# Loading the first two pairs' queries and keys without zeros, and the first loads from one queue

## The chip, the cores and the metric

The program runs on one core of one Trainium2 chip. The metric is device time in microseconds (us) of one execution. TensorE (PE) multiplies, VectorE (DVE), ScalarE (ACT) and GpSimd (POOL) do the elementwise work, and SyncE (SP) issues transfers. SP and ACT each have a queue of transfers of their own; both are served by the same 16 DMA engines.

## The reference

Chunked attention (chunks of 64 rows), and then a mixture of experts on its output:

```python
scores = scale * np.matmul(q_c, k_c.transpose(0, 1, 2, 4, 3))   # (8, 8, 9, 64, 64)
scores = scores - np.max(scores, axis=-1, keepdims=True)
attn = np.exp(scores)
attn = attn / (np.sum(attn, axis=-1, keepdims=True) + 1e-09)
out = np.matmul(attn, v_c)
...
x = np.ascontiguousarray(attn_out.transpose(0, 2, 1, 3)).reshape(B * S, H * D)   # 4608 x 512
expert_idx = np.argmax(x @ w_gate, axis=1)
...   # the 80 tokens of highest gate weight of each of 8 experts
h = np.maximum(x[tok_idx] @ w1[e], 0.0)
out[tok_idx] = gate_w[tok_idx, None] * (h @ w2[e])
```

The change touches only how the first scores are loaded and computed.

## The kernel before

The attention is cut into 18 *pairs* (`NPAIR`); a pair is two tiles of 128 token rows by all 8 heads. For pair n the program runs, in this order of dependence:

- `load_qk(n)`: the queries and keys, 1 MB, in two transfers of 512 KB, into one of three buffers `qb0` to `qb2` (`NB` = 3). The heads' 64 features stand interleaved on even and odd partitions, so that one product with 128 contracted rows gives the scores of two heads. For that the buffer has three stretches of 512 columns, and half the partitions of the two outer stretches hold zeros, written once at the start by `memset`.
- `load_v(n)`: the values, 0.53 MB, in two transfers of 260 KB into `vb0` to `vb2`, whose other halves are zeros too.
- `scores(n)` (L331): 16 products of 128 rows x 64 columns of weights by 128 moving columns in float32, into the PSUM tile `s` (two banks). The trace has two records for each float32 product, so 32 for a pair. Pair 1 borrows the tile tagged `o`.
- `maxima(n)` and `minus(n)` (L348, L353) on DVE, `probs(n)` (L363: 16 transposes on PE into `pt`, then an exponential on ACT into `pT`), `values(2n)`, `values(2n+1)` (L391, into `o`), `divide`, `store` (to `xs`), `xtrans` (L363, `px`), and the gating products (L443).

The loop runs over n and writes the order out by hand, under a manual schedule: each engine does its instructions in the order of the code. In pass n, PE does `scores(n)`, then `xtrans(n-3)`, `values` of pair n-2 and `probs(n-1)`. The loads of pair n+3 are issued on SP in pass n after `scores(n)`, since they go into the buffer that `scores(n)` has just read. A later product on PE therefore waits for whatever stands ahead of it there, and a later transfer for whatever stands ahead of it on SP's queue.

Ahead of the loop stand 25 dummy products (`warm_up(NWARM)`, 128x256 in bfloat16, L664), which use a zeroed tile; pass 1 has 8 more after `probs(0)`. Pair 0 is special: its queries and keys come from `qk0`, an array made in advance that has the zeros in it, in two transfers of 768 KB, one issued by SP and one by ACT (L647). Also at the start SP and ACT share the loads of pairs 1 and 2 and of the first two values; the identity `ident` (64 KB, L648), which `probs` needs, goes on ACT's queue; the other constants go on SP's queue in pass 0. Some lines that the change and the prediction speak of:

```python
for t, eng in enumerate((nc.sync, nc.scalar)):
    eng.dma_start(qbufs[0][:, t], qk0[t])
nc.scalar.dma_start(ident, cst[:, C_ID:C_ID + P])
for j, eng in ((1, nc.vector), (2, nc.gpsimd)):
    eng.memset(qbufs[j][:, :, 0:512], 0.0)
    eng.memset(qbufs[j][:, :, 1024:1536], 0.0)
```

After pair 17 come a selection of tokens (PE, DVE, short dependent steps with dummy products `pwarm`, L620, between them), a gather of the selected rows from `xs` (`xgc`), and the experts: `hc` (L201) and `yc` (L234) on PE, while SP loads 2 MB weights (L905) into buffers as they come free. The expert weights' buffers `w1_0` and `w2_0` (tags `w1`, `w2`) lie empty until pass 15, where `early_weights` begins to fill them.

## Time and profile before

| what | value |
|---|---|
| median of 3 runs | 243.59 us (243.24 to 244.13) |
| profiled execution, its own time | 243.36 us |
| its span (first to last instruction) | 241.6 us |
| PE busy | 222.9 us (92% of the span) |
| DVE, ACT, POOL busy | 114.8, 66.6, 56.6 us |
| moved by DMA | 85.24 MB, mean 353 GB/s |
| on the chain that ended last | PE 85%, DMA 6%, DVE 4% |

The span is 1.8 us shorter than the execution's own time. A busy share is a mean over the program; what a change at the start is worth is read from the first microseconds and from whether PE has idle time behind them.

### The profile page before, as it was taken

Reading aid. Unit: us, or ns where it says so; the run is one execution under the profiler, and the core shown is the slowest. Engines: PE = TensorE matmul, PEld = TensorE weight load, DVE = VectorE, ACT = ScalarE, POOL = GpSimd, SP = SyncE. Lnnn points to the kernel's source line nnn. Section 1 sums busy time; section 2 is a strip of 40 time slices with the busy share of each in tenths; the row PEclk is TensorE's granted clock in tenths of the full one; section 3 lists DMA queues with packets and bytes.
Section 4 is the critical chain, followed back from the end, with each engine's and each line's share of the span. In section 5 each row is a group of like instructions: output and inputs, shape, how many; then the busy total and the mean of one; then the engine's idle time right before and its main releaser. Section 6 shows DMA issues by size and latency. Waiting matters only on the chain.

```text
span 241.6 us, 7213 instructions
## 1 busy us (share of the span) xinstructions
PE 222.9 (92%) x3126; PEld 143.5 (59%) x3126; DVE 114.8 (48%) x250; ACT 66.6 (28%) x117; POOL 56.6 (23%) x158
## 2 busy tenths in 40 slices
PE   8599999999999999989799399999999999999970
PEld 5498988988898898878568233433334333343310
DVE  6468869687878778787586401111211112011210
ACT  0213535363645455454632011201102002010000
POOL 9200400222323222229584620000000000000361
PEclk9999999999999999999979769999999999999997
DMA  6999999999999996989999989999999999999141
GB/s 251 406 382 399 391 407 407 409 410 404 385 379 348 363 346 226 352 322 296 298 409 414 349 250 379 398 407 414 411 401 410 416 408 417 399 403 381 74 151 41
DMA packets 34742, 85.24 MB, mean 353 GB/s; under 512 B 3025, under 2 KB 3153, under 8 KB 34705
## 3 DMA queue, kind: packets, MB, share of 16 engines
q1 hardware_dynamic: 32880, 79.40, 87.0%
q0 software_dynamic: 960, 2.88, 3.5%
q10 hardware_dynamic: 864, 2.43, 2.6%
q8 instruction: 26, 0.43, 0.7%
q14 instruction: 12, 0.09, 0.1%
HBM read 64.53 MB, written 20.45 MB: 352 GB/s over the span
## 4 chain that ended last, share of the span: by engine, by line
PE 85%; DMA 6%; DVE 4%; issue 1%; ACT 1%; POOL 0%; POOLq 0%; DVEq 0%; ACTq 0%
PE hc L201 18%; PE yc L234 17%; PE o L391 14%; PE s L338 13%; PE px L363 5%; PE pt L363 5%; PE small L443 4%; DMA qb<-in_qk 3%; DMA xgc<-xs,gic 3%; PE hpc L219 3%; PE pwarm L620 2%; PE xpc L189 1%; PE small L453 1%; PE small L563 1%; PE two L821 1%
## 5 line engine op out<-in xcount | busy, mean ns | idle before, releaser
L201 PE MATMUL hc<-w,xtc 128*32 128x512 f32 x384 | 45.1, 611 | 0.0
L234 PE MATMUL yc<-w,htc 128*32 128x512 f32 x384 | 42.3, 592 | 0.0
L338 PE MATMUL s<-qb 128*64 128x128 f32 x576 | 35.4, 276 | 2.8 <-DMA qb<-in_qk 2.6
L391 PE MATMUL o<-vb,pT 128*64 128x130 f32 x576 | 36.1, 276 | 0.0
L338 PEld LDWEIGHTS s<-qb 128*64 128x64 f32 x576 | 31.1, 137 | 5.6 <-DVE mx L348 2.4
L391 PEld LDWEIGHTS o<-vb,pT 128*64 128x64 f32 x576 | 31.5, 135 | 1.2
L348 DVE TENSOR_REDUCE mx<-s 128x16 f32<-128x1024 f32 x18 | 22.0, 1225 | 16.7 <-PE s L338 16.6
L234 PEld LDWEIGHTS yc<-w,htc 128*32 128x32 f32 x384 | 12.4, 110 | 28.3 <-issue 28.3
L201 PEld LDWEIGHTS hc<-w,xtc 128*32 128x32 f32 x384 | 12.7, 112 | 26.8 <-issue 25.1
L372 ACT ACTIVATE pT<-pt 128x1024 f32<-128x1024 f32 x18 | 18.4, 1024 | 30.6 <-PE pt L363 30.6
L253 POOL DMA_INDIRECT out<-ysc,to x6 | 6.0, 993 | 88.9 <-SPq L920 86.6
L434 ACT COPY xT<-px 128x1024 f32<-128x1024 f32 x17 | 17.1, 1007 | 22.8 <-PE px L363 22.8
L406 DVE TENSOR_TENSOR x<-o,rc 128x1024 f32<-128x1024 f32 (+1 forms) x20 | 22.4, 1118 | 0.7
L353 DVE TENSOR_TENSOR sm<-s,mx 128x1024 f32<-128x1024 f32 x18 | 22.1, 1227 | 0.6
L206 ACT ACTIVATE hsc<-hc 128x512 f32<-128x512 f32 x6 | 3.6, 598 | 64.9 <-PE hc L201 64.9
L239 DVE TENSOR_SCALAR ysc<-yc,gatec 128x512 f32<-128x512 f32 x6 | 4.5, 751 | 33.5 <-PE yc L234 33.5
L208 DVE TENSOR_SCALAR hsc<-hc 128x512 f32<-128x512 f32 x6 | 4.2, 692 | 26.2 <-PE hc L201 26.2
L223 DVE COPY htc<-hpc 128x512 f32<-128x512 f32 x6 | 4.1, 691 | 22.2 <-PE hpc L219 22.2
L363 PE MATMUL pt<-ct,sm 64*128 64x64 f32 x288 | 12.8, 229 | 1.2 <-ACT pT L372 1.2
L363 PEld LDWEIGHTS pt<-ct,sm 64*128 64x128 f32 x288 | 10.4, 139 | 4.3 <-issue 3.0
L363 PE MATMUL px<-ct,x 64*128 64x64 f32 x288 | 12.8, 229 | 0.0
L543 ACT ACTIVATE lv<-io_b,bo 128x256 bf16<-128x256 bf16 x29 | 12.5, 497 | 0.4 <-DVE bo L523 0.4
(136 smaller groups left out, 210.4 us busy)
## 6 DMA issues: line engine op xcount, KB each, us to landing
w<-in_w SPq DMA_DIRECT2D x12, 2048.0 KB, 18.9
qb<-in_qk SPq DMA_DIRECT2D x32, 512.0 KB, 6.8
out<-zero SPq DMA_DIRECT2D x9, 1024.0 KB, 16.2
vb<-in_vv SPq DMA_DIRECT2D x34, 260.0 KB, 6.4
xs<-x SPq DMA_DIRECT2D x16, 512.0 KB, 6.1
w<-in_w SPq DMA_DIRECT2D x16, 512.0 KB, 7.2
qb<-in_qk ACTq DMA_DIRECT2D x2, 512.0 KB, 8.6
xs<-x SPq DMA_DIRECT2D x4, 256.0 KB, 5.5
```

Of the source, the lines that this page charges most:

```text
L201: nc.tensor.matmul(h[o:o + 32, :], lhsT=xT[r][:, b, o:o + 32], rhs=getw(groups[r][g])[0][:, b, 512 * f:512 * f + 512], start=(b == 0), sto ...
L234: nc.tensor.matmul(y[o:o + 32, :], lhsT=hT[r][c // 4][:, c % 4, o:o + 32], rhs=getw(groups[r][g])[1][:, c, :], start=(c == 0), stop=(c == ...
L338: nc.tensor.matmul(ps[64 * u:64 * u + 64, t, P * pr:P * pr + P].rearrange("p (h k) -> p h k", h=2), lhsT=t8[:, 1, pr, u, :], rhs=t8[:, 0:3 ...
L348: nc.vector.tensor_reduce(d['mx'], d['s8'], axis=AX.X, op=ALU.max)
L353: nc.vector.tensor_tensor(d['sm'].rearrange("p c k h -> p h c k"), d['s8'], d['mx'][:, :, :, None].to_broadcast([P, 2, 8, 64]), op=ALU.sub ...
L363: nc.tensor.transpose(pm[:, u, 64 * c:64 * c + 64], src(c)[rows], ident[rows, rows])
L372: nc.scalar.activation(d['pT'], pt, AF.Exp, scale=0.125)
L391: nc.tensor.matmul(po[64 * u:64 * u + 64, o:o + 130].rearrange("p (h x) -> p h x", h=2), lhsT=d['pT'][:, u, c:c + 64], rhs=v[:, :, pr, u, ...
L406: nc.vector.tensor_tensor(TT[T][:, r:r + nt, :].rearrange("p r (k h e) -> p (r k) h e", k=4, h=2), pov[..., 0:64], rc[:, :, :, None].to_br ...
L434: nc.scalar.copy(dst, pm)
L443: nc.tensor.matmul(pl[32 * j:32 * j + 32], lhsT=wgp[:, pr], rhs=xt[:, 4 * (j % 2) + pr, :], start=pr == 0, stop=pr == 3, tile_position=(0, ...
L543: nc.scalar.activation(lv, io_b, AF.Sign, bias=bo[:, rt:rt + 1], scale=-1.0)
```

## The change

- Pairs 0 and 1 are no longer loaded into `qb0` and `qb1` but, without zeros, into the still empty buffers of expert 0's weights: pair 0 into `w1_0`, pair 1 into `w2_0`, each as two transfers of 512 KB (one for each of the two tiles of rows, `t`). The array `qk0` is gone.
- Their scores are made by 32 products instead of 16: 64 contracted rows x 64 columns of weights by 64 moving columns, at row halves h and column halves u. The scores' tile is laid out by head (`p h (c k)`), and `maxima` and `minus` read it so. The products of t = 0 wait only for the first transfer.
- All loads of the start are issued by SP in the order of use: pair 0, pair 1, `ident`, pair 2, values 0, pair 3, values 1, pair 4, values 2, and then the other constants. Pairs 3 and 4 need not wait for `scores(0)` and `scores(1)` any more. ACT issues none.
- The `memset`s of the buffers are dealt out anew: DVE writes half of `qb2`, `vb0`, both halves of `qb1`; POOL the other half of `qb2`, `qb0`, `vb1`, `vb2`.
- 16 dummy products at the start instead of 25, and 8 more behind `scores(1)`.

The core of the diff:

```diff
-NWARM = 25
+NWARM = 16
...
+        weights[0] = tiles_w(wp, 0)
+        first = {0: weights[0][0][:, 0:2],
+                 1: weights[0][1][:, 0:4].rearrange("p (t w) d -> p t (w d)", t=2)}
+
+        def load_qk(n):
+            if n in first:
+                for t in range(2):
+                    nc.sync.dma_start(first[n][:, t], qk[n, t])
+                return
             for h in range(2):
-                engs[h].dma_start(qbufs[n % NB][h:P:2, :, 512 * h:512 * h + 1024],
+                nc.sync.dma_start(qbufs[n % NB][h:P:2, :, 512 * h:512 * h + 1024],
                                   qk[n, :, 64 * h:64 * h + 64].rearrange("t p f -> p t f"))
...
+            if n in first:
+                for t in range(2):
+                    t8 = first[n][:, t].rearrange("p (w a u s) -> p w a u s", w=2, a=4, u=2)
+                    for pr in range(4):
+                        c = 64 * (4 * t + pr)
+                        for h in range(2):
+                            rows = slice(64 * h, 64 * h + 64)
+                            for u in range(2):
+                                nc.tensor.matmul(
+                                    ps[64 * u:64 * u + 64, h, c:c + 64],
+                                    lhsT=t8[rows, 1 - h, pr, u, :], rhs=t8[rows, h, pr, u, :],
+                                    start=True, stop=True)
+                return
...
-            for t, eng in enumerate((nc.sync, nc.scalar)):
-                eng.dma_start(qbufs[0][:, t], qk0[t])
-            nc.scalar.dma_start(ident, cst[:, C_ID:C_ID + P])
-            for j, eng in ((1, nc.vector), (2, nc.gpsimd)):
-                eng.memset(qbufs[j][:, :, 0:512], 0.0)
-                eng.memset(qbufs[j][:, :, 1024:1536], 0.0)
-            for j, vb in enumerate(vbufs):
-                (nc.vector, nc.gpsimd, nc.gpsimd)[j].memset(vb, 0.0)
+            load_qk(0)
+            load_qk(1)
+            nc.sync.dma_start(ident, cst[:, C_ID:C_ID + P])
+            for j, engs in ((2, (nc.vector, nc.gpsimd)), (0, (nc.gpsimd,) * 2),
+                            (1, (nc.vector,) * 2)):
+                for c, eng in zip((0, 1024), engs):
+                    eng.memset(qbufs[j][:, :, c:c + 512], 0.0)
+                (nc.vector if j == 2 else nc.gpsimd).memset(vbufs[(2, 0, 1).index(j)], 0.0)
             nc.vector.memset(wgp[:, :, 8:32], 0.0)
-            both = (nc.sync, nc.scalar)
-            load_qk(1, both)
-            load_qk(2, both)
-            load_v(0, both)
-            load_v(1, both)
+            for n in range(NB):
+                load_qk(2 + n)
+                load_v(n)
+            nc.sync.dma_start(ct[:, C_ID + P:], cst[:, C_ID + P:])
+            nc.sync.dma_start(wgp[:, :, 0:8], wg.rearrange("(b p) e -> p b e", p=P))
+            nc.sync.dma_start(capi, cap[0:1, :].broadcast_to([P, 2]))
...
                 scores(n)
-                if n + NB < NPAIR:
+                if n == 1:
+                    warm_up(8)
+                if 2 <= n < NPAIR - NB:
                     load_qk(n + NB)
-                    if n == 0:
-                        nc.sync.dma_start(ct[:, C_ID + P:], cst[:, C_ID + P:])
-                        nc.sync.dma_start(wgp[:, :, 0:8], wg.rearrange("(b p) e -> p b e", p=P))
-                        nc.sync.dma_start(capi, cap[0:1, :].broadcast_to([P, 2]))
-                        load_v(2)
```

PE before, from the end of the 25 dummy products to the first of pass 1's eight. `s_159` and `s_187` are the scores of pairs 0 and 1, `qb_99` and `qb_100` the buffers `qb0` and `qb1`, `pt_206` the transposes of pair 0, `ct` holds the identity; `DMAHW0` to `DMAHW7` are the semaphores that the transfers use in turn, and the other waits are for an engine.

```order
L338 MATMUL s_159<-qb_99 64x128 [waits DMAHW1_49]
L338 MATMUL s_159<-qb_99 64x128 x7
L338 MATMUL s_159<-qb_99 64x128 [waits DMAHW0_49]
L338 MATMUL s_159<-qb_99 64x128 x7
L338 MATMUL s_187<-qb_100 64x128 [waits DMAHW4_49,DMAHW3_49,DVE_49]
L338 MATMUL s_187<-qb_100 64x128 x15
L363 MATMUL pt_206<-ct,sm_185 128x64 [waits DMAHW2_49,DVE_49]
L363 MATMUL pt_206<-ct,sm_185 128x64 x15
```

PE of the change, from the end of its 16 dummy products. `s_163` and `s_200` are the scores of pairs 0 and 1, `w_0_102` and `w_0_103` the weights' buffers `w1_0` and `w2_0`.

```order
L350 MATMUL s_163<-w_0_102 64x64 [waits DMAHW0_49]
L350 MATMUL s_163<-w_0_102 64x64 x15
L350 MATMUL s_163<-w_0_102 64x64 [waits DMAHW1_49]
L350 MATMUL s_163<-w_0_102 64x64 x15
L350 MATMUL s_200<-w_0_103 64x64 [waits DMAHW2_49]
L350 MATMUL s_200<-w_0_103 64x64 x15
L350 MATMUL s_200<-w_0_103 64x64 [waits DMAHW3_49]
L350 MATMUL s_200<-w_0_103 64x64 x15
L687 LDWEIGHTS warm
L687 MATMUL small<-warm 128x256
```

Twice the products, each pair in two halves that wait for one transfer each, no wait for DVE's zeros ahead of pair 1, and a first dummy product where the transposes of pair 0 stood (they now follow the eight dummy products, and eight more follow them).

SP before, its first transfers. `vb_102` and `vb_103` are the values' buffers.

```order
L647 DMA qb_99<-in_qk 128x1536
L320 DMA qb_100<-in_qk 64x2x1024 [waits DVE_49]
L320 DMA qb_101<-in_qk 64x2x1024 [waits Pool_49]
L328 DMA vb_102<-in_vv 64x2x520 [waits DVE_49]
L328 DMA vb_103<-in_vv 64x2x520 [waits DMAHW1_49,Pool_49]
L320 DMA qb_99<-in_qk 64x2x1024 [waits DMAHW3_49,DMAHW0_49,PE_49]
```

SP of the change, its first transfers.

```order
L325 DMA w_0_102<-in_qk 128x1024 x2
L325 DMA w_0_103<-in_qk 128x1024 x2
L670 DMA ct<-in_cst 128x128
L328 DMA qb_101<-in_qk 64x2x1024 [waits DVE_49]
L328 DMA qb_101<-in_qk 64x2x1024 [waits Pool_49]
L336 DMA vb_104<-in_vv 64x2x520 [waits DVE_49]
L336 DMA vb_104<-in_vv 64x2x520 [waits DMAHW0_49]
L328 DMA qb_99<-in_qk 64x2x1024 [waits DMAHW1_49,Pool_49]
L328 DMA qb_99<-in_qk 64x2x1024 [waits DMAHW2_49,Pool_49]
```

SP now issues both halves of each load, the first five wait for nothing, and from the ninth transfer on each waits for the one eight places ahead of it to land. `qb_99` (pair 3) no longer waits for PE.

## Rows read from the trace of the kernel before

**Rows 1.** Chain of waits, first 21 us: start us, length us, what.

```profile
2.08 0.92 DVE qb L651
3.02 7.96 DMA qb<-in_qk
11.12 1.97 PE s L338 x32
13.09 0.65 PE pt L363 x16
13.74 0.98 PE small L664 x8
14.71 1.92 PE s L338 x32
...
17.92 1.23 DVE sm L353
...
19.25 1.97 PE s L338 x32
```

**Rows 2.** Windows: us, then busy us of PE, PEld, DVE, ACT, POOL; clock, DMA share, GB/s.

```profile
0.00:4.00 4.00, 2.91 (x14) 2.04 (x15) 2.45 (x3) 0.00 (x0) 3.47 (x8) 1.00 0.49 158
4.00:8.00 4.00, 3.64 (x32) 2.51 (x31) 1.27 (x2) 0.00 (x0) 3.38 (x6) 1.00 1.02 416
8.00:12.00 4.00, 1.81 (x34) 1.60 (x32) 2.45 (x2) 1.79 (x3) 0.00 (x0) 1.00 1.02 408
12.00:16.00 4.00, 4.00 (x68) 3.48 (x66) 2.45 (x2) 1.02 (x1) 0.00 (x0) 1.00 1.06 406
16.00:20.00 4.00, 3.78 (x74) 3.50 (x72) 3.24 (x5) 0.93 (x1) 0.00 (x0) 1.00 1.03 356
20.00:25.00 5.00, 5.00 (x99) 4.52 (x96) 4.33 (x6) 1.58 (x3) 0.00 (x0) 1.00 1.02 395
30.00:40.00 10.00, 10.00 (x195) 8.96 (x189) 7.55 (x12) 4.15 (x6) 0.00 (x0) 1.00 1.04 408
94.00:96.00 2.00, 2.00 (x46) 1.93 (x44) 1.88 (x6) 1.42 (x3) 0.23 (x2) 1.00 0.30 66
```

**Rows 3.** Timeline, first 18 us: start us, length, engine, line, what, count, idle before.

```profile
1.09 5.51 PE L664 MATMUL small<-warm 128*128 128x256 bf16 x25 [1.09 <-POOL warm L645]
3.38 1.79 DVE L653 MEMSET vb<- 128x2080 f32 x1 [0.38 <-issue]
...
6.96 1.97 PE L338 MATMUL s<-qb 128*64 128x128 f32 x32 [0.36 <-DMA qb<-in_qk]
...
8.98 1.22 DVE L348 TENSOR_REDUCE mx<-s 128x16 f32<-128x1024 f32 x1 [3.71 <-PE s L338]
...
13.67 1.05 PE L664 MATMUL small<-warm 128*128 128x256 bf16 x8
```

**Rows 4.** DMA view, first 1.3 us: issues, KB each, us to landing.

```profile
qb<-in_qk SPq DMA_DIRECT2D x1, 768.0 KB, 6.2
qb<-in_qk ACTq DMA_DIRECT2D x1, 768.0 KB, 6.4
```

**Rows 5.** Line L320, ACT's second issue (pair 2): issue, then issue to landing.

```profile
L320 ACTq DMA_DIRECT2D qb<-in_qk x1: 614/614/614, 3.8 to 3.8; - x1
...
DMA to landing us min/median/max: 9.2/9.2/9.2
```

**Rows 6.** Line L320, SP's issue at 11.0 us (pair 3, second half).

```profile
L320 SPq DMA_DIRECT2D qb<-in_qk x1: 602/602/602, 11.0 to 11.0; - x1
...
DMA to landing us min/median/max: 7.9/7.9/7.9
```

**Rows 7.** Chain of waits, later pieces: gating products, the gather, the experts.

```profile
29.53 1.01 PE small L443 x32
...
131.53 7.30 DMA xgc<-xs,gic
...
140.09 5.17 PE hc L201 x32
...
154.31 3.57 PE hc L201 x32
...
210.74 3.67 PE hc L201 x32
```

**Rows 8.** Windows: the two stretches of half clock, and the experts.

```profile
122.75:126.16 3.41, 3.39 (x17) 2.17 (x16) 2.82 (x5) 0.81 (x3) 2.92 (x8) 0.50 1.02 408
136.40:143.20 6.80, 4.19 (x20) 1.50 (x24) 0.60 (x4) 0.74 (x2) 3.35 (x5) 0.50 0.80 238
160.00:210.00 50.00, 50.00 (x464) 17.22 (x456) 6.40 (x9) 5.28 (x9) 0.00 (x0) 1.00 1.04 411
```

**Rows 9.** Waits of SP's queue: waiting line, what ended it, total us, times, longest.

```profile
SPq L905 <- DVE w L904: 14.9, 2, 14.5
```

More of the change, by code (lines that the diff above doesn't have):

```diff
@@ L54, in attention_moe @@
 @with_exitstack
-def attention_moe(ctx: ExitStack, tc: tile.TileContext, qk, qk0, vv, wg, w1, w2, cap, cst, out):
+def attention_moe(ctx: ExitStack, tc: tile.TileContext, qk, vv, wg, w1, w2, cap, cst, out):
     nc = tc.nc
@@ L316, in attention_moe @@
                  for j in range(NB)]
-        def load_qk(n, engs=(nc.sync, nc.sync)):
+        weights[0] = tiles_w(wp, 0)
[6 more added lines that the diff above has]
+                return
             for h in range(2):
-                engs[h].dma_start(qbufs[n % NB][h:P:2, :, 512 * h:512 * h + 1024],
+                nc.sync.dma_start(qbufs[n % NB][h:P:2, :, 512 * h:512 * h + 1024],
                                   qk[n, :, 64 * h:64 * h + 64].rearrange("t p f -> p t f"))
@@ L324, in attention_moe, with load_v @@
                  for j in range(NB)]
-        def load_v(n, engs=(nc.sync, nc.sync)):
+        def load_v(n):
             for h in range(2):
-                engs[h].dma_start(vbufs[n % NB][h:P:2, :, h],
+                nc.sync.dma_start(vbufs[n % NB][h:P:2, :, h],
                                   vv[n, :, h].rearrange("t p f -> p t f"))
@@ L346, in maxima @@
             d['mx'] = wk.tile([P, 2, 8], F32, name=f"mx{n}", tag="mx")
-            d['s8'] = d['s'].rearrange("p t (c h k) -> p h (t c) k", h=2, k=64)
+            d['s8'] = (d['s'].rearrange("p h (c k) -> p h c k", k=64) if n in first else
+                       d['s'].rearrange("p t (c h k) -> p h (t c) k", h=2, k=64))
             nc.vector.tensor_reduce(d['mx'], d['s8'], axis=AX.X, op=ALU.max)
@@ L632, in early_weights @@
             e, c = divmod(n, 8)
-            if c == 0:
+            if n == 8:
                 weights[e] = tiles_w(wp, e)
@@ L1044, in _arrays @@
         [np.where(f, k, q), np.where(f, q, k)], -1).reshape(NPAIR, 2, P, QK))
-    a = r["qk"][0].reshape(2, 2, 64, QK)
-    z = np.zeros((2, 64, 2, QK + 512), a.dtype)
-    z[:, :, 0, :QK], z[:, :, 1, 512:] = a[:, 0], a[:, 1]
-    r["qk0"] = z.reshape(2, P, QK + 512)
     r["vv"] = np.ascontiguousarray(t.reshape(NPAIR, 2, 2, 64, VW))
```

## Prediction

> **What bounds the kernel now.** I read the windows first, to see whether PE ever has time to make up a late or early start. It has none: from 30 to 40 us and from 160 to 210 us PE is busy for the whole stretch, and so it is already from 12 us on, but for a moment near 19 us [rows 2, 8]. So what happens before PE's row of work begins goes one for one into the end. Then the chain of waits shows where that row begins [rows 1]. Zeros written by DVE until 3.0 us hold back a load of pair 1 that ACT issues; it lands at 10.98 (3.02 + 7.96), and from its landing on everything is PE: scores of pair 1 at 11.12, transposes of pair 0, eight dummy products, scores of pair 2 at 14.71. Scores of pair 3 come 4.54 us later, held by DVE's subtraction for pair 2. Ahead of 11 us PE has idle time: 1.81 of 4 us busy from 8 to 12 [rows 2]. **The mark I follow is the start of pair 2's scores, 14.71 us**; behind it the order of work is the same before and after.
>
> The second thing is the DMA. It moves 416, 408, 406 GB/s from 4 to 16 us, full [rows 2]. So the landings of the start are bytes in order over this rate, and I need their curve.
>
> **The curve of the bytes.** From rows 2 (GB/s by length): 0.63 MB by 4 us, 2.30 by 8, 3.93 by 12, 5.55 by 16, 6.98 by 20. A transfer has landed somewhat after the bytes up to its own are through, since later ones run beside it. Three landings give that lag. Pair 0 (2 x 0.79 = 1.57 MB) lands at 0.72 + 6.2 to 6.4 = about 7.0 [rows 4], where the curve has 1.88: lag 0.3 MB. Pair 2 lands at 3.8 + 9.2 = 13.0 [rows 5] with 4.33 MB moved; ahead of it and with it stand 1.57 + 0.07 + 1.05 + 1.05 = 3.74: lag 0.6. Pair 3 lands at 18.9 [rows 6] with 6.58 moved against 5.85 (another 1.05 and two values of 0.53): lag 0.7.
>
> **Loads after.** In the new order the sums in MB are: pair 0 0.52 and 1.05, pair 1 1.57 and 2.10, identity 2.16, pair 2 3.21, values 3.74, pair 3 4.79, values 5.33, pair 4 6.38, values 6.91. With the lag they land, by the curve, at about 4.4 and 5.7, 7.2 and 8.5, 8.7, **11.5 (pair 2)**, 13.0, 15.8, 17.4, 20.3, 22. Pair 2 comes 1.5 us earlier than before, nearly all of it the 0.52 MB of zeros no longer loaded (1.3 us at 0.41 MB/us). SP's own time does not bind: nine issues at 0.6 us each [rows 5] end by about 6 us, while the bytes of the first eight last until 13. Waiting for the transfer eight places ahead leaves over 2 MB, some 5 us, in the queues.
>
> **PE after.**
> - *Dummy products.* 16 instead of 25 at 0.22 us [rows 3] end at 1.09 + 3.5 = 4.6 us. Nothing is saved by that on the path, since pair 0's first half lands at 4.4; kept at 25 they would hold pair 0 until 6.6, and it would still be done about when pair 1 lands.
> - *The 64-row products.* The trace has none. Bounds for a pair (64 records): the same columns stream as in 32 records of 128 columns, which take 1.97 us [rows 3]; the gating products take 1.01 us for 32 records of a quarter of the columns of the array [rows 7], so 2.0 for 64; if two row halves ran beside each other as the column halves do, 1.0; if each record cost what a 128-column one does, 3.9. Two rows say 2.0, and I take it: 1.0 for a half.
> - *Pair 0* is done at 5.7 + 1.0 = 6.7. DVE's zeros, now 3 x 0.92 + 1.79 + 0.14, with gaps, end near 6.2 and just miss being late. Maxima and subtraction (1.22 + 1.23 [rows 1, 3]) are ready at 9.2, the identity at 8.7, both over 1 us ahead of the transposes below.
> - *Pair 1* is done at 8.5 + 1.0 = 9.5. Behind it stand eight dummy products (0.98), the transposes of pair 0 (0.65), eight dummy products (0.98) [rows 1]: 2.6 us, **pair 2's scores at 12.1**. The new eight are a cost of 1 us on the path, partly covered: without them the transposes would start at 9.5 and pair 2 at its landing, 11.5.
> - *Behind it*, by the spacing of before: values 0 at 13.8 (landed 13.0), pair 3 at 16.6 (15.8), values 1 at 19.3 (17.4), pair 4 at 21.7 (20.3). Each load is there, pair 3 and values 0 by only 0.8 us. The constants go from ahead of values 2 to behind it and land near 23; the first to want them is ACT's copy near 23, which nothing on PE waits for at once.
>
> **The sum.** 14.71 - 12.1 = 2.6 us earlier. The other edits (layout of the scores, POOL's zeros, which gate only loads that land after 11 us) are hidden behind the loads. The profiled execution took 243.36: 243.36 - 2.6 = 240.8. The median of the runs is 0.23 above it, so **241.0 us**. With products at 1.0 us for a pair the chain is 11.6, just behind pair 2's landing: 3.1 us, 240.5. With 3.9 it is 13.1: 1.6 us, 242.0.
>
> TensorEngine Tiling (Array Packing) of the Trainium skill, section Tiling Modes, says that 64x64 tiles are four independent ones that load and multiply in parallel. By it the products take the 1.0 us end and the time is 240.5; no run here shows it.
>
> **Does the gain last to the end?** The DMA has room before the experts (share 0.30 from 94 to 96 us [rows 2]), so its stream moves with PE. The experts' weights are loaded once the gather has landed (the wait of 14.5 us [rows 9]), and the gather moves along too.
>
> **Rivals.**
> - *The clock, which is also the case that ends slower.* The first 25 dummy products take 0.22 us each, the later eight 0.13 [rows 3]. 256 columns at 1.2 GHz are 0.21 us, at 2.4 GHz 0.11: PE starts at the lower level, though the window prints 1.00, and has risen by pair 0's scores, 1.97 us as in all later pairs. Before, 5.5 us of unbroken work stood ahead of the rise. Now 3.5 us do, and then halves of pairs with gaps for loads. If PE is still at 1.2 GHz through pair 1, its half costs 2.0 and not 1.0, and part of the dummy products doubles: 1 to 1.6 us lost, 242.0 to 242.6. At half clock up to pair 2's scores the chain is 8.5 + 2 x 3.6 = 15.7, 1.0 later than before: 244.6. It decides near 14 us: a rise later than that makes the kernel slower, by half of every further us. For it: PE stands at 0.50 in two later stretches, one of them behind its wait for the gather [rows 7, 8]. Against: the gap of over 2 us before pair 1 did not bring it down [rows 2, 3]. TensorE: Matmul & The Clock Gate of the Trainium skill, Part 1, has the throttled state as the default, released by sustained activity at a point that differs between runs; that speaks against cutting the warm-up, and the trace's slow start agrees. 0.16 for the small loss, 0.04 for slower.
> - *The loads decide.* If pair 2 lands no earlier than before (13.0), because one queue starts slower than two, the scores start at 13.1 and the gain is 1.6: 242.0. For it: pair 2, pair 3 and values 0 have under 1 us to spare. Against: from 30 to 40 us SP alone carries 408 GB/s. 0.10.
> - *Given back in the experts.* The DMA carries 411 GB/s from 160 to 210 us, and one piece of `hc` at 210.74 takes 3.67 instead of 3.57 us [rows 7, 8]: a weight comes just in time. If that stream did not move, PE would wait for it there and the time would be 243.5. Against it stands what I said of the gather. 0.08.
> - *Luck behind the start.* Pieces at half clock (5.17 us instead of 3.57 for `hc` [rows 7]) may fall otherwise when all moves by 2.6 us: about 1 us either way. This only widens the range.
>
> **Chances.** Forecast 0.62 (240.0 to 241.6). Measuring tells apart about 0.5%, 1.2 us, so faster means below 242.4: the forecast, the loads' case and two thirds of the small clock loss, 0.83. Same: the rest of that and the experts' case, 0.13. Slower 0.04. The range reaches from the 1.0 us products with some luck (239.9) to the clock's small loss (242.6).
>
> **What the profile after will show.** Pair 0's products start near 4.6 us, pair 1's end near 9.5, pair 2's scores start between 11.5 and 12.5, and pair 2's loads land near 11.5. Later pieces of the chain stand 2.6 us earlier with equal spacing; 64 records of a pair's products take 1 to 2 us without their wait. I am wrong if dummy products behind pair 1 take 0.2 us each (the clock), if PE waits for a load at pair 2 or 3, or if the shift of the experts' first piece is smaller than that of pair 2's scores.

## The result, and the profile after

The changed kernel takes 241.04 us (median of 4 runs, 240.1 to 242.63), the kernel before on the same chip 243.86 (4 runs, 243.24 to 244.78): ratio 0.9885, 95% interval 0.984 to 0.993. It was run again later, beside other kernels: 241.99 against 244.58, 0.9892 (0.9851 to 0.9932). So it is faster by 1.1%, by the medians 2.8 and 2.6 us. The profiled execution took 240.75 (span 238.9), against 243.36 (span 241.6); the spans differ by 2.7 us. All ratios here go by undisturbed runs and all medians by all runs; e6, e7, e8 and e9 below had disturbed ones among theirs.

The chain of waits after, for the first 18 us and three later places (start, length, what), stands against [rows 1, 7]:

```profile
2.11 7.02 DMA w<-in_qk
9.13 0.04 issue
9.17 0.69 PE s L350 x32
9.87 0.98 PE small L687 x8
10.85 0.65 PE pt L385 x16
11.49 0.98 PE small L687 x8
12.47 1.90 PE s L359 x32
...
17.11 1.97 PE s L359 x32
...
27.40 1.01 PE small L465 x32
...
111.85 1.01 PE small L465 x32
...
130.48 6.28 DMA xgc<-xs,gic
...
137.92 4.85 PE hc L201 x32
...
151.83 3.57 PE hc L201 x32
...
208.26 3.46 PE hc L201 x32
```

The chain has the predicted form: the landing of pair 1's second half at 9.13, its products, eight dummies, transposes, eight dummies, **pair 2's scores at 12.47 instead of 14.71**. The loads view of SP gives the landings (issue plus its time to landing): pair 0 at 4.31 and 5.52, pair 1 at 7.87 and 9.13, identity 9.35, pair 2 at 10.60 and 11.89, values 0 by 14.02, pair 3 at 15.32 and 16.61.

PE's timeline shows the four halves of the 64-row products; the bracket is the idle time ahead, and what ended it:

```profile
4.36 0.69 PE L350 MATMUL s<-w 64*64 64x64 f32 x32
5.56 0.69 PE L350 MATMUL s<-w 64*64 64x64 f32 x32 [0.51 <-DMA w<-in_qk]
7.92 0.69 PE L350 MATMUL s<-w 64*64 64x64 f32 x32 [1.66 <-DMA w<-in_qk]
9.17 0.69 PE L350 MATMUL s<-w 64*64 64x64 f32 x32 [0.56 <-DMA w<-in_qk]
```

Each half (32 records) takes 0.69 us, and each but the first waits for its transfer. The windows, against [rows 2]:

```profile
4.00:8.00 4.00, 1.83 (x72) 1.27 (x73) 3.64 (x6) 0.00 (x0) 4.00 (x5) 1.00 0.98 356
8.00:12.00 4.00, 3.44 (x94) 2.83 (x95) 2.84 (x3) 0.98 (x3) 0.27 (x2) 1.00 1.02 396
12.00:16.00 4.00, 4.00 (x69) 3.67 (x66) 1.97 (x3) 0.56 (x1) 0.00 (x0) 1.00 1.03 409
```

PE is still half idle up to 8 us, but busy from 9 on, except for 0.2 us near 17. The DMA moved 356 GB/s from 4 to 8 us, where it was 416 before.

**Where the 2.7 us of the spans are** is not a straight line. Take the shift of each place against before: pair 2's scores 14.71 - 12.47 = 2.24; gating products 29.53 - 27.40 = 2.13 [rows 7]. Those of the last tokens stood here in the chain of before:

```profile
113.07 1.01 PE small L443 x32
```

113.07 - 111.85 is only 1.22: 0.91 us has been lost in between, in the loop over the pairs. The gather starts 131.53 - 130.48 = 1.05 us sooner, but takes 6.28 instead of 7.30 us, which gives 1.02 back; the later pieces of `hc` are 2.17, 2.48 and 2.48 us ahead, and the last of them is 0.2 shorter (3.46 for 3.67), as the prediction's rows had a weight just in time there. The two places of the loss show on PE's timeline after:

```profile
39.82 1.42 PE L359 MATMUL s<-qb 128*64 128x128 f32 x21
41.49 0.87 PE L359 MATMUL s<-qb 128*64 128x128 f32 x11 [0.26 <-issue]
...
48.30 2.33 PE L413 MATMUL o<-vb,pT 128*64 128x130 f32 x32
```

Scores, which take 1.97 us elsewhere on this timeline, stop after 21 of 32 records, with no semaphore to wait for; with the stop they last 2.54 us. By the starts of the values' products behind them (44.75 before, 43.20 after) 0.58 us is lost here. The other 0.33 is in the values' products at 48.30, which take 2.33 us instead of 2.00. The experiments with more 64-row products show what kind of stop this is.

### The profile page after: what moved, and what is told of

Its sections match the earlier page's. It is cut to its first block, busy times and chain, and to the rows that moved or that the text cites. A ratio compares the mean times of both kernels' runs of the same rounds, so it can differ in the third digit from the quotient of the medians.

```text
span 238.9 us, 7340 instructions
## 1 busy us (share of the span) xinstructions
PE 220.6 (92%) x3189; PEld 141.1 (59%) x3189; DVE 115.5 (48%) x251; ACT 66.7 (28%) x117; POOL 57.4 (24%) x159
## 4 chain that ended last, share of the span: by engine, by line
PE 87%; DMA 6%; DVE 2%; ACT 1%; issue 1%; SPq 1%; POOL 0%; POOLq 0%; DVEq 0%; ACTq 0%
PE hc L201 18%; PE yc L234 17%; PE o L413 15%; PE s L359 13%; PE pt L385 5%; PE px L385 5%; PE small L465 4%; DMA w<-in_qk 3%; DMA xgc<-xs,gic 3%; PE hpc L219 3%; PE pwarm L642 1%; PE xpc L189 1%; PE small L585 1%; PE small L475 1%; PE two L841 1%
## 5 line engine op out<-in xcount | busy, mean ns | idle before, releaser
L201 PE MATMUL hc<-w,xtc 128*32 128x512 f32 x384 | 44.6, 608 | 0.0
L413 PE MATMUL o<-vb,pT 128*64 128x130 f32 x576 | 36.4, 276 | 0.0
L359 PE MATMUL s<-qb 128*64 128x128 f32 x512 | 31.8, 276 | 0.5 <-issue 0.3
L359 PEld LDWEIGHTS s<-qb 128*64 128x64 f32 x512 | 27.7, 137 | 2.9 <-issue 1.4
L201 PEld LDWEIGHTS hc<-w,xtc 128*32 128x32 f32 x384 | 12.1, 112 | 26.9 <-issue 26.2
L565 ACT ACTIVATE lv<-io_b,bo 128x256 bf16<-128x256 bf16 x29 | 12.5, 497 | 0.4 <-DVE bo L545 0.4
```

The source lines that it names most:

```text
L201: nc.tensor.matmul(h[o:o + 32, :], lhsT=xT[r][:, b, o:o + 32], rhs=getw(groups[r][g])[0][:, b, 512 * f:512 * f + 512], start=(b == 0), sto ...
L359: nc.tensor.matmul(ps[64 * u:64 * u + 64, t, P * pr:P * pr + P].rearrange("p (h k) -> p h k", h=2), lhsT=t8[:, 1, pr, u, :], rhs=t8[:, 0:3 ...
L413: nc.tensor.matmul(po[64 * u:64 * u + 64, o:o + 130].rearrange("p (h x) -> p h x", h=2), lhsT=d['pT'][:, u, c:c + 64], rhs=v[:, :, pr, u, ...
L565: nc.scalar.activation(lv, io_b, AF.Sign, bias=bo[:, rt:rt + 1], scale=-1.0)
```

## The experiments

Theory: the bytes ahead of pair 1's last landing, and then 3.3 us of PE, set the start; 64-row products are cheap because four of them run at once. Rivals: that only the order of loads matters, that one queue is slow, that the clock decides, that the gain is lost later. The table has medians, with the ratio to the kernel before on the same chip; the two times in the middle are those of the profiled execution (in e2, e4, e7 and e9 the start is PE's timeline's, which can be 0.07 us earlier than that of the chain of waits).

| kernel | pair 1 landed, us | pair 2's scores start, us | median, us | ratio (95%) |
|---|---|---|---|---|
| before | 10.98 | 14.71 | 243.86 | 1 |
| changed | 9.13 | 12.47 | 241.04 | 0.9885 (0.984 to 0.993) |
| changed, again | 8.25 | 12.69 | 241.99 | 0.9892 (0.9851 to 0.9932) |
| e1 order of loads alone | 9.60 | 13.33 | 242.84 | 0.9925 (0.9894 to 0.9956) |
| e2 two queues | 8.47 | 13.13 | 241.56 | 0.9900 (0.9864 to 0.9936) |
| e3 without the new eight | 8.98 | 12.62 | 240.85 | 0.9861 (0.9809 to 0.9913) |
| e4 25 dummies | 8.12 | 11.60 | 240.65 | 0.9840 (0.9805 to 0.9875) |
| e5 no dummies | 8.32 | 12.78 | 241.89 | 0.9890 (0.9859 to 0.9921) |
| e6 one quadrant at a time | 9.17 | 13.36 | 242.58 | 0.9890 (0.9838 to 0.9943) |
| e7 all 18 pairs | 8.37 | 11.63 | 248.30 | 1.0142 (1.009 to 1.0193) |
| e8 four pairs | 9.29 | 15.16 | 243.72 | 0.9952 (0.992 to 0.9983) |
| e9 four pairs, 25 dummies | 9.19 | 12.46 | 242.70 | 0.9920 (0.9882 to 0.9957) |
| e10 half of pair 1 left out | 7.32 | 11.13 | 239.37 | 0.9788 (0.9755 to 0.9822) |
| e11 all pairs, half the loads | 5.68 (its one half) | 10.10 | 232.80 | 0.951 (0.9475 to 0.9545) |

**e1: the order of the loads alone**, with zeros, 128-row products and 25 dummies as before.

```
-for t, eng in enumerate((nc.sync, nc.scalar)):
-    eng.dma_start(qbufs[0][:, t], qk0[t])
+for t in range(2):
+    nc.sync.dma_start(qbufs[0][:, t], qk0[t])
...
-load_qk(1, both)
-load_qk(2, both)
-load_v(0, both)
-load_v(1, both)
+load_qk(1)
+nc.sync.dma_start(ident, cst[:, C_ID:C_ID + P])
+load_qk(2)
+load_v(0)
...
```

Values 1 and 2 are loaded in passes 0 and 1, the other constants in pass 1.

> The kernel before with the order of the first loads alone: SP issues all of them in order of use (pair 0 with its zeros, pair 1, identity, pair 2, values 0, and then as before, constants last); products, zeros and 25 dummy products as before. My theory, that landings are bytes in order over the DMA rate: pair 1 needs 2.6 MB plus a lag of 0.4, which at the rates seen in the changed kernel are through at about 10.1 us (before 10.98), so pair 2's scores start near 13.7 instead of 14.7: 1.0 us faster, ratio 0.996. Rival, that the gain comes from the zeros not loaded and the new products alone, or that one queue starts slower than two: no change or slower, ratio 1.000 to 1.004.

Pair 1 landed at 9.60, 1.4 us sooner than before, and pair 2's scores began at 13.33:

```profile
3.02 6.58 DMA qb<-in_qk
...
13.33 1.92 PE s L338 x32
```

So of the 2.24 us at the mark the order alone gives 1.4, more than the 1.0 expected. The other 0.9 is, by the rows, 0.5 of earlier landing (9.13 for 9.60), 1.3 of shorter products behind it (0.69 for 1.97) and 0.1 of a shorter gap between the two, less 1.0 for the eight new dummies. The time cannot be told from the changed kernel's: 0.9925 (0.9894 to 0.9956) stands against 0.9885 and 0.9892, whose intervals overlap it. e1's DMA moved 416 GB/s from 4 to 8 us from SP's queue alone, so one queue can carry that rate, here with transfers of 768 KB first.

**e2: the changed kernel with SP and ACT sharing the first loads.**

```
-load_qk(0)
-load_qk(1)
...
+both = (nc.sync, nc.scalar)
+load_qk(0, both)
+load_qk(1, both)
...
```

> The changed kernel, but pairs 0, 1 and 2, the identity and values 0 are shared by SP's and ACT's queues, one half each. The changed kernel moved 356 GB/s from 4 to 8 us where the kernel before moved 416, and pair 1 landed at 9.13 us, not at 8.5 as I had worked out. If one queue alone is why, two queues bring the 416 back, pair 1 lands near 8.5 and the time falls by 0.6 us: ratio 0.986 against 0.9885. If the queue is not why (both queues use the same engines), pair 1 still lands near 9.1 and the ratio stays at 0.988 to 0.989; halves that take turns would bring the first half of a pair later and the second no earlier.

The time is no better, though the rate (419 GB/s from 4 to 8 us) and pair 1's landing (8.47) came as the theory had them. What the landing gained was lost behind it. The clock fell to 0.50 (1.2 GHz) from 8.2 to 11.6 us, so that pair 1's products and the eight dummies took 1.79 and 1.89 us, and from landing to mark it was 4.7 us instead of 3.3:

```profile
7.91 1.79 PE L350 MATMUL s<-w 64*64 64x64 f32 x64 [1.18 <-DMA w<-in_qk]
9.63 1.89 PE L688 MATMUL small<-warm 128*128 128x256 bf16 x8
```

And ACT's half of values 0 waited for DVE's zeros ahead of its issue, and PE waited 0.26 us for it:

```profile
5.77 9.34 DMA vb<-in_vv
...
15.35 1.99 PE o L413 x32
```

That the second queue brought the early landing is not shown: the changed kernel's second profile, below, has 8.25 with one queue and 403 GB/s.

**e3: without the new eight dummies** behind pair 1's scores.

```
 scores(n)
-if n == 1:
-    warm_up(8)
```

> The changed kernel without the eight dummy products behind pair 1's scores. By my sum they stand on the path: the transposes of pair 0 start at 9.8 instead of 10.8, pair 2's scores as soon as they have landed (11.89), near 12.0 instead of 12.4: 0.4 us faster, ratio 0.987. Rival, the clock: without them PE is too idle from 6 to 10 us, the clock falls or does not rise, and what follows is slower by up to 1.5 us: ratio 0.990 to 0.995.

In the profiled execution nothing was gained at the mark (12.62): the clock fell to 0.50 (1.2 GHz), and a half of pair 1 took 1.13 us:

```profile
8.66:12.07 3.41, 3.04 (x53) 2.56 (x54) 1.99 (x3) 1.33 (x3) 0.00 (x0) 0.50 1.03 409
```

The fall began at 8.66, while the eight would have begun behind pair 1's scores, at 9.7 or later, so leaving them out did not cause it; it came in e2 and in e8 too, which have them. The time, with an interval of 0.981 to 0.991, cannot be told from the changed kernel's, and whether the eight cost what the expectation says stays open.

**e4: 25 dummies ahead of pair 0 instead of 16.**

```
-NWARM = 16
+NWARM = 25
```

> The changed kernel with 25 dummy products ahead of pair 0 again instead of 16. My theory, that the landing of pair 1's second half (9.13 us) decides when pair 2's scores begin: the 25 end at about 5.6 us (16 end at 4.36, nine more at about 0.13 us each once the clock has risen), pair 0's scores shift by 1.2 us into the idle 1.66 us ahead of pair 1's, and nothing moves at pair 2's scores: 12.5 us, ratio to the changed kernel 1.000 +- 0.002 (ratio to the kernel before about 0.988). Rival, that the fewer dummies themselves were worth time: pair 2's scores at 13 us or later and the run 0.5 to 1 us longer than the changed kernel.

```profile
1.09 5.19 PE L687 MATMUL small<-warm 128*128 128x256 bf16 x25 [1.09 <-POOL warm L667]
6.21 1.63 PE L350 MATMUL s<-w 64*64 64x64 f32 x96
8.16 0.70 PE L350 MATMUL s<-w 64*64 64x64 f32 x32 [0.33 <-DMA w<-in_qk]
```

The extra nine end at 6.2, ahead of pair 1's landing, and cost nothing: the landing decides. It came at 8.12 here. That is no effect of the dummies: the changed kernel's second profile has 8.25, and nine executions with the same first four loads spread from 8.12 to 9.29 (four below 8.4, five above 8.9). The mark came at 11.60, not at the 12.5 expected. Of the 3.1 us 0.26 went to a wait for values 0 at 13.83; the other 2.85 held to the end of the loop, and nothing was lost at 41 us.

**e5: no dummies ahead of pair 0.**

```
-NWARM = 16
+NWARM = 0
```

> The changed kernel without the dummy products ahead of pair 0 (the eight behind pair 1's scores stay). My theory, that the dummies before the first landing are what raises TensorE's clock before the scores come: without them the clock is at 0.50 until some microseconds into the scores, a half of pair 0's or pair 1's products takes 1.1 us as it did in the half-clock stretch of the run without the eight, pair 2's scores begin 1 to 2 us later than 12.47 us and may themselves run at half speed; 242 to 244.5 us. Rival, that the landing decides and the clock has time to rise between 4.4 and 9.1 us: pair 2's scores at 12.5 us, 240.5 to 241.5 us.

```profile
4.61 3.58 PE L350 MATMUL s<-w 64*64 64x64 f32 x96 [4.61 <-DMA w<-in_qk]
8.36 1.13 PE L350 MATMUL s<-w 64*64 64x64 f32 x32 [0.17 <-DMA w<-in_qk]
9.43 1.73 PE L687 MATMUL small<-warm 128*128 128x256 bf16 x8
```

A half takes 1.13 and eight dummies 1.73 us, until about 11 us. These are the times of a clock of 0.50 (1.13 us is what a half took at 0.50 in e3), though the windows print 1.00 here, as they do at the start of every run. From landing to mark it is 12.78 - 8.32 = 4.46 us instead of 3.34. That is the small clock loss of the prediction, at 0 dummies and not at 16; it ends before the scores of pair 2. The mark came 0.3 us behind the changed kernel's instead of the 1 to 2 expected, since pair 1 landed 0.8 us sooner, and the time, at a ratio of 0.989, is not told from that of the changed kernel.

**e6: the same products in another order**, four in a row on one quadrant of the array.

```
-for pr in range(4):
-    c = 64 * (4 * t + pr)
-    for h in range(2):
-        rows = slice(64 * h, 64 * h + 64)
-        for u in range(2):
+for h in range(2):
+    rows = slice(64 * h, 64 * h + 64)
+    for u in range(2):
+        for pr in range(4):
+            c = 64 * (4 * t + pr)
```

> The changed kernel with the same 64-row products of pairs 0 and 1 issued in another order: four in a row that use the same quadrant of the array, instead of four that use the four different quadrants. Theory that the 0.69 us of a half comes from four quadrants at work at once: a half now takes 1.6 to 2.2 us (32 products one behind the other at the 50 to 70 ns apart of the other products), pair 1's second half ends 1.0 to 1.4 us later, pair 2's scores at about 13.6 us, ratio to the kernel before 0.993. Rival, that a product of 64x64 is simply short whatever stands beside it: 0.69 us a half and a ratio of 0.988 as in the changed kernel.

```profile
7.94 2.81 PE s L350 x63
```

A half costs 1.4 us instead of 0.69, and pair 2's scores begin at 13.36. So the products are cheap when neighbours use different quadrants. The times cannot show the 0.9 us (interval 0.984 to 0.994). TensorEngine Tiling (Array Packing) of the Trainium skill, section Tiling Modes, has 64x64 tiles as four independent ones: the trace agrees (0.69 against 1.4 us).

**e7: all 18 pairs by 64-row products**, no zeros in the queries' buffers at all.

```
-if n in first:
+if True:
+    b = first.get(n, qbufs[n % NB])
     for t in range(2):
-        t8 = first[n][:, t].rearrange(...
+        t8 = b[:, t, 0:QK].rearrange(...
```

> The changed kernel with all 18 pairs by 64-row products: all loads of queries and keys without the stretched layout, in two transfers of one tile of rows each, no zeros in their buffers. A pair's products took 32 records in 0.53 us (0.69 with the tail) for a half in the changed kernel, so 1.1 to 1.3 us for a pair instead of 1.97. If PE's row of work is what sets the attention's pace (5.9 us a pair), each of 16 pairs saves 0.7 to 0.8 us until the DMA sets it: 2.1 MB a pair at 0.405 MB/us are 5.2 us. Then 16 x 0.7 = some 9 to 11 us less: 230 to 232 us, ratio 0.945 to 0.955, with PE waiting for loads in the attention. Rival: the DMA, with little room in the first 60 us, or DVE takes most of it: 3 to 6 us, 235 to 238. If switching the array between ways of splitting it cost much, the products would take 2 us as before and nothing is gained.

Slower than before by 1.4%, though the products are busy for less time. The page's groups, of the changed kernel and of this one (busy, mean ns, then idle time ahead and what ended it):

```profile
L359 PE MATMUL s<-qb 128*64 128x128 f32 x512 | 31.8, 276 | 0.5 <-issue 0.3
```

```profile
L347 PE MATMUL s<-qb 64*64 64x64 f32 x1024 | 20.6, 222 | 6.9 <-issue 6.7
```

20.6 instead of 31.8 us of products, but 6.7 us of idle time inside them that no semaphore explains, and 6.4 more in the two kinds of transposes (`px` and `pt`). On the timeline the pieces stop at odd counts:

```profile
30.69 0.68 PE L347 MATMUL s<-qb 64*64 64x64 f32 x26
32.72 0.81 PE L347 MATMUL s<-qb 64*64 64x64 f32 x38 [1.35 <-issue]
```

Counting the records of PE and PEld (its few semaphore instructions among them) in order of time, the stops of 0.7 us and more that no semaphore explains, up to 100 us, stand within one record of 450, 706, 1218, 1474, 2498, 3010, 3778, 4034 and 4290: each a multiple of 256 behind 194. What comes in such steps is the queue of kind instruction:

```profile
q8 instruction: 27, 0.44, 0.7%
```

```profile
q8 instruction: 31, 0.51, 0.8%
```

The changed kernel has 27 such packets (6378 products and weight loads, some 25 x 256), this one 31 (7402, some 29 x 256). Narrow windows of the DMA view place each packet: in e7 at about 11.2, 17.5, 23.5, 30.2 and 36.4 us, 6.0 to 6.7 us apart, and PE goes on 2.3 to 2.6 us behind the first two and the last two of them (13.48, 20.10, 32.72, 38.79).

**e8: four pairs**, with 16 dummies; **e9**: the same with 25.

```
+2: weights[0][0][:, 2:4],
+3: weights[0][1][:, 4:8].rearrange("p (t w) d -> p t (w d)", t=2)}
```

> The changed kernel with the same treatment for pairs 2 and 3 too (64-row products from the free halves of the two weights' buffers; the zeroed buffers are used from pair 4 on). Theory that a pair's products take about 1.2 us in this form instead of 1.97 us wherever PE is the engine that is waited for: pair 2's scores begin at 12.4 us as now and end 0.7 us sooner, pair 3's begin at its first half's landing and end 1.3 us sooner than now (17.8 against 19.08 us); if the spacing behind stays, the run gains 1.0 to 1.5 us on the changed kernel, 239.5 to 240.1 us, ratio to the kernel before 0.983. Rival, from the run with all 18 pairs in this form, whose PE stood idle 1.3 us and more at almost every 256th of its records (1218, 1474, 2498 and so on), some 2.3 us behind a packet on the queue of kind instruction, with the next packet never less than 6.0 us behind the one before: instructions come no faster than 256 in about 6 us, so what the pairs gain is waited for at the next such mark (records 450 and 706), pair 4's scores begin where they did, and the time is that of the changed kernel, 240.8 to 241.2 us.

Two things went wrong in e8. The clock fell to 0.50 from 8.7 to 15.5 us (this window begins and ends a little sooner):

```profile
8.30:15.10 6.80, 6.21 (x99) 4.28 (x89) 3.24 (x3) 1.53 (x3) 0.02 (x1) 0.53 1.03 409
```

and PE stopped for 1.36 us in pair 3's scores, at record 706 as the rival said:

```profile
19.07 1.15 PE s L352 x61
20.22 1.36 issue
21.58 0.33 PE s L352 x3
```

> Pairs 0 to 3 by 64-row products, with 25 dummies ahead of pair 0 instead of 16. With 16 dummies the four pairs took 243.7 us: TensorE's clock fell to 0.50 from 8.3 to 15.1 us, pair 2's scores began 2.7 us late, and PE stood idle 1.36 us inside pair 3's scores at its record 706. Theory clock alone: with 25 dummies it stays up as in the kernel with two pairs and 25 dummies, pair 2's scores begin at 11.6 to 12.5 us and the shorter products of pairs 2 and 3 gain 0.7 to 1.3 us on that kernel's 240.65: 239.3 to 240.0 us, ratio to the kernel before 0.980. Theory instructions: the clock stays up, but record 706 comes no sooner than 5.6 to 6.0 us behind record 450, so that PE waits 0.8 to 1.4 us in pair 3's scores or right behind them, pair 4's scores begin where they did, and the time is 240.4 to 241.2 us, ratio 0.984 to 0.986.

With the clock up in e9 pair 2's scores begin at 12.46 and take 1.16 instead of 1.97 us, and the stop remains:

```profile
16.47 1.03 PE L352 MATMUL s<-w 64*64 64x64 f32 x52
18.38 0.45 PE L352 MATMUL s<-w 64*64 64x64 f32 x12 [0.88 <-issue]
```

So the theory of the clock alone fails: what the products save is waited for at the next mark, as that of the instructions says. Its figure does not hold, though: record 706 came 5.4 us behind record 450 (18.38 and 13.00), not 5.6 to 6.0, and that packets are never less than 6.0 us apart, as the expectation of e8 has it, is true of the first five packets of e7 alone; the next four come 4.4 to 5.6 us apart. The time fits neither theory: at 0.992 it is even longer than the changed kernel's, and the profiled execution (241.26) does not show why.

**e11: e7 with half its loads**: the second half of each pair's queries and keys and of its values is not loaded; its products read the first half, and half of the values are zeros.

```
-for t in range(2):
+for t in range(1):
     nc.sync.dma_start(b[:, t, 0:QK], qk[n, t])
...
-for h in range(2):
+for h in range(1):
     nc.sync.dma_start(vbufs[n % NB][h:P:2, :, h],
```

> All 18 pairs by 64-row products, with half the loads left out: only the first half of each pair's scores data and of its values is loaded (1.3 MB a pair with the stores instead of 2.1), the products of the second half read the first half's data and half of the values stay zero, so the results are not the reference's. With all loads this form took 248.3 us, PE idle for 1.3 us and more at nearly every 256th of its records. Theory that packets of instructions wait behind the data's: with room on the transfer engines the packets come in 3 to 4 us behind their request, the idle stretches mid-scores go, a pair takes 5.3 us and record 3778 is reached 5 us or more sooner than 84.8 us; 238 to 243 us. Rival, that 256 records cannot follow in under 5.6 us whatever the load: idle stretches and record 3778 as before, within 2 us, and 246 to 248.5 us.

The windows of e7 and of e11 up to record 3778:

```profile
0.00:84.77 84.77, 72.57 (x1870) 62.52 (x1871) 58.06 (x93) 32.02 (x49) 18.82 (x66) 0.96 0.98 360
```

```profile
0.00:74.30 74.30, 67.88 (x1874) 58.83 (x1875) 57.84 (x94) 31.94 (x49) 18.74 (x66) 1.00 0.80 253
```

The same work is done 10.5 us sooner, with 253 GB/s instead of 360, of which up to 3.4 (an estimate) is e7's two stretches at half clock of 3.4 us each; 4.7 us less of busy PE and 5.8 less of idle. A packet starts some time after PE has passed the mark 256 records ahead of the one that needs it: in e7 3.4 to 4.2 us at the marks of the first 35 us and 2.0 to 3.1 at those from 38 to 54, in e11 1.0 to 1.8 from 22 to 48. The changed kernel's second profile has such a difference within itself. At record 1474 (42.05 us) the DMA moves over 400 GB/s and the packet starts 4.7 us behind the mark; at record 3522 (93.90 us) it moves nothing, and the packet starts at 94.25, 0.35 us behind:

```profile
93.90:94.25 0.35, 0.35 (x10) 0.35 (x10) 0.35 (x1) 0.34 (x1) 0.00 (x0) 1.00 0.00 0
```

So **instructions wait behind the data's transfers**, and with fewer of those most stops go. The rate alone does not set how long: e7 moves over 400 GB/s also where its packets take 2.0 and 2.5 us. A few stops remain in e11 (1.40 us at 11 us, 0.79 at 22, 0.48 and 0.65 between 54 and 61), each behind a packet that started 2.7 to 4.0 us behind its mark.

The loss in the changed kernel is the same thing. The table has record 1218, the start of the packet behind it (the window of 0.25 us that it falls in begins there, so that the delay is at least the one given), and where PE was with record 1474:

| kernel | record 1218, us | packet, us | behind it, us | record 1474 |
|---|---|---|---|---|
| changed | 34.86 | 39.0 | 4.1 | PE idle from 41.24 to 41.49 |
| changed, again | 35.13 | 39.25 | 4.1 | PE idle from 41.52 to 42.05 |
| e10 | 33.57 | 37.75 | 4.2 | PE idle from 39.95 to 40.48 |
| e3 | 35.44 | 38.75 | 3.3 | no stop |
| e4 | 33.59 | 36.5 | 2.9 | no stop |
| e6 | 35.74 | 38.25 | 2.5 | no stop |

PE needs 6.0 us for these 256 records, and where it stops it goes on some 2.5 us behind the packet's start: a start 3.3 us behind the mark was in time, one of 4.1 was not. The second loss is the next mark: in the changed kernel the packet behind record 1474 starts between 46.0 and 46.25 us, at least 4.5 us late, and record 1730 comes at 48.64, within the values' products shown above. Before, the delay was 2.6 to 3.3 us at the marks between 33 and 47 us, and no stop is seen up to 105 us. e2 and e6 have the changed kernel's instruction count and did not stop, so this belongs to an execution and not to the count alone. What delays the packet in some of them stays open: the changed kernel and e4 move 407 and 409 GB/s from 34 to 42 us alike.

**e10: half of pair 1's load left out**; its products read the first half twice.

```
-for t in range(2):
+for t in range(2 - n):
     nc.sync.dma_start(first[n][:, t], qk[n, t])
```

> The changed kernel with the second half of pair 1's load left out (512 KB; its products read the first half's data instead, so pair 1's scores are not the reference's). Theory that the bytes ahead of pair 1's last landing set the start: everything behind lands 1.2 to 1.3 us sooner (the spacing of the halves), pair 2's scores begin at 11.2 us instead of 12.47, and the run is 1.1 to 1.3 us shorter than the changed kernel: ratio to it 0.995, to the kernel before 0.983. Rival, that the chain of PE, DVE and ACT from pair 0 on sets it: less than 0.4 us.

```profile
1.64 5.68 DMA w<-in_qk
...
11.13 1.90 PE s L359 x32
```

The mark moved to 11.13, where 11.2 was expected, and not by less than 0.4 us as the rival has it: the bytes ahead of pair 1 are the bound of the start. The median is 2.6 us below that of the changed kernel beside it, 1.7 below its first; the mark gives 1.3 to 1.6 of that, and where the rest comes from is not shown. (Its profiled execution lost 1.2 us at records 1474 and 1730, and took 240.64.)

**The changed kernel again.**

> The changed kernel itself again, beside the other kernels of this call, so that they stand against it on one chip: ratio to the kernel before 0.985 to 0.990 (0.9885 was measured). Its profile is a second sample of the first loads: the landing of pair 1's first half has come at 6.8 to 7.1 us in three kernels with this load order (25 dummies, none, all pairs in the new form) and at 7.8 to 8.0 us in four, the changed kernel among them. If that scatter belongs to the execution and not to the kernel, it may land at either; at 6.8 to 7.1 us pair 2's scores begin at about 11.7 us instead of 12.47.

Here the first half of pair 1 landed at 6.99 and the second at 8.25, but pair 2's second half 2.8 us behind its first:

```profile
4.08 8.47 DMA qb<-in_qk
...
12.69 1.97 PE s L359 x32
```

So the scatter belongs to the execution. Pair 0's products differ too: they took 1.93 us instead of 2 x 0.69, most of it as long as at the lower clock, which did not matter, since they ended at 6.5, ahead of pair 1's landing. A hole of 1.1 us beyond the 1.3 that a half takes stood ahead of pair 1 in the first profile, and one of 1.5 us within pair 2 in this one: the marks, 12.47 and 12.69, are near each other.

## Why the prediction was right, and where only the sum was

The time, 241.0 predicted and 241.04 measured (a gain of 2.6 us predicted, 2.8 and 2.6 by the medians of the two sets of runs), came out of several steps, some of them off in opposite directions. The mechanism of the start is right; that the sum comes out to the tenth is luck.

- **What bounds the start** held: a landing, then PE without a gap. e10 shows it by 512 KB, e4 by dummies that cost nothing.
- **The bytes' curve** gave pair 0 at 4.4 and 5.7 (measured 4.31, 5.52), pair 1 at 7.2 and 8.5 (7.87, 9.13), identity 8.7 (9.35), pair 2 11.5 (11.89), values 0 13.0 (14.0), pair 3 15.8 (16.6). From pair 1 on it was 0.4 to 1.0 us early. The curve of before was used at its 416 GB/s, and 356 was moved; the predicted 8.5 for pair 1 lies inside the 8.12 to 9.29 of nine executions. What makes the hole stays open: the early and the late ones have the same order and the same one queue, and e1 moved 416 GB/s from one queue. That the zeros no longer loaded are nearly all of what is earlier, as the prediction says of pair 2, does not hold for pair 1, which decides: with the zeros still loaded, the order alone brought it from 10.98 to 9.60 (e1), and pair 2 from 12.93 to 12.35.
- **The 64-row products** were mis-sized: 1.0 us a half taken, 0.69 measured (1.16 for a whole pair without a wait, e9), near the end of 1.0 us for a pair. e6 shows why. This took back 0.3 of the late landing: mark 12.47 for a predicted 12.1, 2.24 us gained instead of 2.6.
- **Dummies**: 16 ended at 4.4 (predicted 4.6), on no path. The new eight do stand on the path, with 0.98 us in the chain of waits; what leaving them out would gain was not shown, as the clock fell in e3.
- **"Behind it, by the spacing of before"** is the step that failed: 0.91 us was lost at two places of the loop, in scores and in values' products, at the marks of late packets of instructions, which neither the sum nor a rival had. The loads named there as close (pair 3, values 0) did come in time, with PE idle only for 0.2 us at 17 us, as before. One of the prediction's own signs of being wrong shows the loss: the experts' first piece shifts by 2.17 us, less than the 2.24 of pair 2's scores, and by 1.15 without the gather's gain. Another, a wait for pair 2, came in the second profile.
- **The luck behind the start**, given as about 1 us either way for pieces at half clock, made up for that loss, but mostly by something else. The pieces at half clock gave 0.3 us (the first `hc` 4.85 for 5.17), the weight that came just in time 0.2, and the gather 1.0 (6.28 for 7.30), which the prediction had nowhere. The gather takes 7.3 us in the profiles of before, e1, e8 and e9 and 6.3 to 6.5 in the ten others, the changed kernel's two among them. Why is not known, nor whether it goes by the execution or by the kernel. Without it the two spans would differ by 1.7 us instead of 2.7.
- **Rivals.** The clock's small loss is real, but came with fewer dummies (e5) or with a fall in three profiles (e2, e3, e8), and in neither of the changed kernel's two. That loads decide: half true, since pair 2's landing at 12.56 set the mark in the second profile, at 12.69; but with the same one queue it came at 11.89 in the first. Given back in the experts: no, their pieces shift by 2.2 to 2.7.

A version that surely beats the changed kernel was not found. 25 dummies (0.984) has the lowest time among those that compute everything, but the intervals overlap, on different chips.

## What to carry to other kernels

Where the start is a chain from a load, count the bytes ahead of the last load that PE waits for; here the order of use alone gave 1.4 of the 2.24 us at the mark. Small products on different quadrants of the array run side by side (a half in 0.69 instead of 1.4 us, a pair in 1.16 instead of the 1.97 of 128-row products), but there are twice as many instructions. On this kernel, whose transfer engines are full, a saving on PE was only had where 256 records still lasted longer than a packet of instructions took to come: in e7's first 35 us 3.4 to 4.2 us from the mark to its start, and some 2.5 more until PE went on. An idle "issue" in the midst of equal products is the sign to look for, and the place to count records.

## What was not expected of the hardware

- PE can stop at a 256th record (PE and PEld together) whose packet of instructions is late; packets started up to 4.7 us behind their mark with the DMA at over 400 GB/s (the changed kernel's second profile), 1.0 to 1.8 with about 257 (e11, 22 to 48 us), and 0.35 with none.
- The changed kernel lost 0.9 us at such marks in one execution and 1.2 in another; e2 and e6, with as many instructions, did not stop.
- TensorE can be back at 0.50 (1.2 GHz) at 8.7 us, after a half of pair 1 at full speed (0.69 us, e3). How long PE was busy ahead of it does not tell alone: of the stretch from 4 to 8 us it was 2.47 us in e3, and 1.83 in the changed kernel, which kept the higher level.
- Transfers of the same order at the start land up to 1.2 us apart in different executions.
